# Two half transfers change places, and three weight pieces are loaded as 8 and 120 rows

## The chip, the cores and the metric

The kernel runs on one core of a Trainium2 chip. A core has a matrix engine (TensorE; PE in the profile, with its weight loads as PEld), a vector engine (VectorE, DVE), an activation engine (ScalarE, ACT), a general engine (GpSimd, POOL) and a small engine that mostly issues transfers (SyncE, SP). Transfers are carried by the core's 16 DMA engines. The metric is the device time of one execution in microseconds, the median over the runs; lower is better.

## The reference

Attention with a threshold, and after it a feed-forward block with a SoLU activation. All is in single precision; the two weight matrices come in double precision.

```python
# q, k, v: (8 batches, 8 heads, 576 tokens, 64)
scores = q @ k.T / sqrt(64)
thresh = max(scores, axis=-1) - tau
scores = where(scores >= thresh, scores, -1e9)
attn = exp(scores - max(scores)); attn /= sum(attn) + 1e-9
x = (attn @ v)            # heads side by side: (4608 tokens, 512)
h = x @ w_in              # (4608, 1024)
solu = h * softmax(h)
ln = (solu - mean) / sqrt(var + 1e-6) * g_ln
out = ln @ w_out          # (4608, 512)
```

## The kernel before

**Slots and units.** The attention is cut into slots. A slot is one batch, one kind (0 and 1 are the two large parts of the tokens, 2 the rest), one pair of heads and one of two row blocks r. Two slots, r = 0 and 1, make a unit. A loop runs over rounds; round `rnd` writes down the scores of slot `rnd` and, besides, the later steps of earlier slots. There is no scheduler behind it: each engine gets its instructions in the order in which this loop writes them.

In a slot, TensorE makes the scores (`scores`, L480), VectorE the row minima (`maxes`, L502), ScalarE applies the threshold (`ramp`, L517) and the exponential (`exps`, L526), and GpSimd divides by the sums (`normalise`, L533 to L536). In the next round VectorE transposes the two blocks into a tile `T` (`blocks`, L548).

**The transfers of a unit.** When both slots of a unit are in `T`, three DMAs on SyncE's queue bring it into the tile `wT`, in which the heads are arranged as the next product needs them: L557 takes the 64 middle partitions of `T` into all 128 partitions of `wT` (its second group of columns), and L559, in a loop over `half`, takes partitions 0 to 31 of `T` into rows 0 to 63 of `wT` (half 0) and partitions 96 to 127 into rows 64 to 127 (half 1). L564 is the form of kind 2, with four transfers. There are two buffers of `wT`.

**The product behind them.** Three or four rounds later (`LAG_PV`) `attend_steps` writes the matmuls of `pv`, L590: for each of nine blocks m first those that read rows 0 to 63 of `wT` (u = 0), then those of rows 64 to 127 (u = 1). `attended` copies the result on ScalarE (L622) into `xh`, from which the feed-forward steps go on: `ff_h` (L645, L655), `ff_max` and `ff_exp`, `ff_stats`, `ff_swap` (four DMAs, L737), `ff_turn` and `ff_o` (L760). In the steady part the rounds interleave this work with the scores on TensorE.

**The weights.** The double-precision weights are loaded in 16 pieces of 128 rows of 512 numbers (4096 bytes a row) by `weight_load(x)`, L275: pieces 0 to 2 on ScalarE's queue, the others on SyncE's. `weight_a`, `weight_b` and `weight_c` turn a piece into single precision on VectorE, ScalarE and GpSimd, one piece a round in rounds 0 to 15; `weight_d` (L332) brings the output weights with their row halves changed round into a second place. In round r, behind the unit's transfers, piece r + 4 is loaded (in round 0 pieces 3 and 4, in round 11 none, in round 12 piece 15). So pieces 5, 8 and 11 are issued in rounds 1, 4 and 7, and between them stand loads of the values `v` (L177, L182).

**SyncE's queue.** SyncE issues its DMAs one after the other, each when what it needs is there. The completion of DMAs is told by eight semaphores in turn, and a DMA waits until the one eight before it, which used the same semaphore, has landed.

Of the kernel before, what the change touches and what calls it, by code (L numbers as in the profile page):

```python
# [16 lines left out]
P = 128  # L17
# [3 lines left out]
def kernel(  # L21
# [236 lines left out]
    def piece(x):  # L258
        if x < 2 * NP:
            c, hf = divmod(x, 2)  # L260
            cols = slice(512 * hf, 512 * hf + 512)
            return w_in[P * c : P * c + P, cols], w1[:, c, cols], W_UNIT
        c = x - 2 * NP
        return w_out[P * c : P * c + P], w2[:, 2 * c], gs[:, c : c + 1]
# [4 lines left out]
    def weight_load(x):  # L269
        raw = work.tile(  # L270
            [P, 512], I64 if wide else F32, tag=("xh2", "xh3", "uT", "xh1")[x % 4 if x < 15 else 0],
            bufs=1, name="raw"
        )
        queue = nc.scalar if x < 3 else nc.sync
        queue.dma_start(out=raw, in_=piece(x)[0])  # L275
        raws[x] = dict(raw=raw)

    def weight_a(x):
# [261 lines left out]
    def blocks(s):  # L540
        b, kind, hp, r = slots[s]
        key = (b, kind, hp)
        if r == 0:
            units[key] = dict(T=work.tile([P, NB, 2, 2, 32], F32, tag="T", name="T"))
        u = units[key]
        T = u["T"]
        for h, w in enumerate(live.pop(s)["w"]):
            nc.vector.transpose(out=T[:, :, r, h, :], in_=w)  # L548
        if r == 0:
            return  # L550


        T = T.rearrange("p (c m) r h x -> p c (m r h x)", c=2)
        u["wT"] = wT = work.tile([P, 2, NK, 2, 2, 32], F32, tag="wT", bufs=2, name="wT")
        to = wT.rearrange("p g m r h x -> p g (m r h x)")
        if kind < 2:
            nc.sync.dma_start(out=to[:, 1], in_=T[32:96])  # L557
            for half in range(2):
                nc.sync.dma_start(out=to[ROWS[half], 0], in_=T[96 * half : 96 * half + 32])  # L559
            return  # L560
        for g in range(2):
            for half in range(2):
                of = 64 * half + 32 * g
                nc.sync.dma_start(out=to[ROWS[half], g], in_=T[of : of + 32])  # L564
# [303 lines left out]
    with tc.manual_schedule():  # L868
        nc.scalar.dma_start(out=tau_t, in_=tau.partition_broadcast(P))
        load_qk(0, 0)  # L870
        weight_load(0)
        constants()
        for x in range(1, 3):
            weight_load(x)
# [23 lines left out]
        while True:  # L898
# [135 lines left out]
            if rnd - 1 in live:  # L1034
                blocks(rnd - 1)
# [10 lines left out]
            if rnd in pieces:  # L1046
                x = pieces[rnd]
                weight_b(x)
                for y in {0: (3, 4), 11: (), 12: (15,)}.get(x, (x + 4,)):
                    if y < len(pieces):  # L1050
                        weight_load(y)
                if x + 1 < len(pieces):
                    weight_a(x + 1)
# [39 lines left out]
```

## Time and profile before

| what | value |
|---|---|
| median of 3 runs | 868.01 us (865.58 to 868.37) |
| profiled execution | 869.02 us, its span 867.2 us |
| mean granted TensorE clock | 0.976 |
| instructions | 36122 |
| TensorE busy | 822.9 us, 95% of the span |
| SyncE's DMA queue (q1) | 82416 packets, 164.25 MB |
| `wT<-T` issues of L557 and L559, and of L564 | 64 of 576 KB; 160 of 288 KB |
| loads of weight pieces (`raw`) on SyncE | 5 and 8 of 512 KB |

Times in the views are in microseconds from the start of the span. A line of the view in order of time gives the start, the length, the engine, the line of the kernel, what is done, how often, and in brackets how long the engine stood idle before and what ended that. "SPq" is an issue on SyncE. The granted clock is the share of full speed that TensorE was allowed. A pass is one matmul instruction as the profile counts it.

### The profile page before, as it was taken

What the parts mean: (1) busy time and instruction counts of PE and PEld (TensorE: products, weight loads), DVE (VectorE), ACT (ScalarE), POOL (GpSimd) and SP (SyncE); (2) the same over time, 40 slices, a digit from 0 to 9 for tenths busy, and PEclk for the clock granted to TensorE, in tenths of its full rate; (3) what the DMA queues carried; (4) which work ended last, traced back from release to release, by engine and by line L of the source; (5) the groups of instructions that cost most, each with busy time, mean ns of one, the idle gap of its engine ahead of it and who ended that gap; (6) DMA issues with size and microseconds to landing.
All of it is one profiled execution on the core that took longest, in us unless ns stands there. A gap on an engine that the chain in (4) does not pass through costs nothing.

```text
span 867.2 us, 36122 instructions
## 1 busy us (share of the span) xinstructions
PE 822.9 (95%) x15361; PEld 605.8 (70%) x15361; DVE 681.7 (79%) x1248; ACT 573.6 (66%) x1153; POOL 500.2 (58%) x938
## 2 busy tenths in 40 slices
PE   5668799989999999999999999999999999999997
PEld 3446466667677776899777766777777777777655
DVE  4988878878788888888888887888788887787361
ACT  5877876667677767777666766777677776776121
POOL 2886656556756666565656665565666655555120
PEclk9769999999999999999999999999999999999999
DMA  8999887998888878898888787888788787655312
GB/s 256 252 251 227 191 210 181 210 236 210 215 206 226 208 183 214 208 221 203 196 207 225 207 187 185 217 220 207 183 230 229 197 192 180 163 136 139 69 38 62
DMA packets 83712, 168.54 MB, mean 194 GB/s; under 512 B 15448, under 2 KB 45152, under 8 KB 83552
## 3 DMA queue, kind: packets, MB, share of 16 engines
q1 hardware_dynamic: 82416, 164.25, 76.3%
q8 instruction: 120, 1.97, 1.0%
q10 hardware_dynamic: 1136, 2.00, 0.7%
q14 instruction: 40, 0.33, 0.1%
HBM read 46.14 MB, written 9.44 MB: 64 GB/s over the span
## 4 chain that ended last, share of the span: by engine, by line
PE 79%; DMA 8%; DVE 4%; ACT 4%; SPq 2%; issue 2%; POOL 1%; ACTq 0%; DVEq 0%
PE o_ps L760 26%; PE h_ps L655 20%; PE pv L590 14%; PE s_ps L480 14%; DMA wT<-T 6%; PE h_ps L645 3%; ACT w L517 1%; DVE w L502 1%; ACT w L526 1%; DVE T L548 1%; DMA q<-in_q_dram 1%; DMA qT<-flip 1%; SPq L564 1%; DMA k<-in_k_dram 1%; SPq L559 0%
## 5 line engine op out<-in xcount | busy, mean ns | idle before, releaser
L760 PE MATMUL o_ps<-w,uT 64*64 64x256 f32 x4608 | 271.6, 378 | 1.2 <-ACT xe L622 0.6
L502 DVE CUSTOM_DVE_ANT_0 w<-s_ps,tau_t 128x576 f32<-128x576 f32 x280 | 200.0, 751 | 90.0 <-PE s_ps L480 61.6
L517 ACT ACTIVATE w<-s_ps,nth 128x576 f32<-128x576 f32 x280 | 196.9, 739 | 107.0 <-DVE nth L502 89.6
L760 PEld LDWEIGHTS o_ps<-w,uT 64*64 64x64 f32 x4608 | 212.7, 134 | 66.1 <-ACT xh L622 12.1
L536 POOL TENSOR_SCALAR w<-w,sm 128x576 f32<-128x576 f32 x288 | 222.1, 783 | 14.3
L548 DVE STREAM_TRANSPOSE T<-w 128x576 f32<-128x576 f32 x288 | 207.6, 755 | 20.6 <-POOL w L536 19.1
L655 PE MATMUL h_ps<-w,xh 64*64 64x512 f32 x1856 | 221.0, 589 | 0.1
L526 ACT ACTIVATE w<-w,ntau 128x576 f32<-128x576 f32 x288 | 219.7, 767 | 0.0
L590 PEld LDWEIGHTS pv<-wT,v 64*64 64x64 f32 x5760 | 175.2, 138 | 45.4 <-issue 24.5
L480 PE MATMUL s_ps<-kT,qT 64*64 64x64 f32 (+1 forms) x2048 | 177.1, 422 | 13.3 <-ACT w L517 10.9
L590 PE MATMUL pv<-wT,v 64*64 64x128 f32 (+1 forms) x5760 | 178.0, 266 | 10.9 <-DMA wT<-T 7.8
L655 PEld LDWEIGHTS h_ps<-w,xh 64*64 64x64 f32 x1856 | 118.0, 133 | 78.8 <-issue 45.7
L533 POOL TENSOR_SCALAR sm<-sm 128x2 f32<-128x2 f32 x144 | 37.0, 257 | 201.8 <-ACT w L526 198.5
L534 POOL TENSOR_TENSOR sm<-sm,mone 128x2 f32<-128x2 f32 x144 | 108.7, 755 | 12.0
L480 PEld LDWEIGHTS s_ps<-kT,qT 64*64 64x64 f32 x2048 | 73.0, 139 | 21.7 <-ACT w L517 15.7
L622 ACT COPY xh<-pv 128x256 f32<-128x256 f32 x64 | 25.1, 393 | 82.4 <-PE pv L590 82.4
L721 ACT ACTIVATE V<-u,nb,rs 128x1024 f32<-128x1024 f32 x36 | 44.7, 1241 | 39.3 <-POOL nb L711 32.4
L747 DVE STREAM_TRANSPOSE uT<-V 128x1024 f32<-128x1024 f32 x36 | 44.2, 1227 | 18.1 <-DMA V<-u 17.7
L526 ACT ACTIVATION_READ_ACCUMULATOR w<-w,ntau 128x1 f32 x288 | 55.6, 193 | 0.0
L685 DVE TENSOR_TENSOR u<-h_ps,u 128x1024 f32<-128x1024 f32 x36 | 42.8, 1190 | 9.8 <-ACT u L679 9.8
L726 DVE TENSOR_SCALAR u<-u,rs,nb 128x1024 f32<-128x1024 f32 x36 | 35.3, 982 | 17.6 <-ACT V L721 17.6
L670 DVE TENSOR_REDUCE hm<-h_ps 128x1 f32<-128x1024 f32 x36 | 42.9, 1192 | 4.8 <-PE h_ps L645 2.7
(90 smaller groups left out, 568.1 us busy)
## 6 DMA issues: line engine op xcount, KB each, us to landing
wT<-T SPq DMA_DIRECT2D x160, 288.0 KB, 6.7
wT<-T SPq DMA_DIRECT2D x64, 576.0 KB, 5.4
V<-u SPq DMA_DIRECT2D x144, 64.0 KB, 3.3
out_dram<-ob SPq DMA_DIRECT2D x71, 128.0 KB, 2.5
q<-in_q_dram SPq DMA_DIRECT2D x24, 288.0 KB, 5.7
qT<-flip SPq DMA_DIRECT2D x48, 144.0 KB, 4.2
k<-in_k_dram SPq DMA_DIRECT2D x24, 288.0 KB, 6.1
kT<-flip SPq DMA_DIRECT2D x48, 144.0 KB, 3.9
```

Source lines behind the costliest of these rows:

```text
L480: nc.tensor.matmul(out=ps[h][ROWS[y], ks], lhsT=lhsT, rhs=d["kT"][ROWS[h], ks], start=True, stop=True,)
L502: nc.vector.tensor_tensor_reduce(out=w, in0=ps[:, 0:S], in1=(zero if loose else tau_t).to_broadcast([P, S]), scale=1.0, scalar=BIG, op0=AL ...
L517: nc.scalar.activation(out=d["w"][x], in_=d["w"][x] if d["loose"] else d["ps"][x][:, 0:S], func=AF.Prelu, bias=d["nth"][x], scale=-1.0, al ...
L526: nc.scalar.activation(out=w, in_=w, func=AF.Exp, bias=ntau, scale=1.0, accum_out=sm[:, x : x + 1])
L534: nc.gpsimd.tensor_tensor(out=sm, in0=sm, in1=mone, op=ALU.pow)
L536: nc.gpsimd.tensor_scalar(out=w, in0=w, scalar1=sm[:, x : x + 1], scalar2=1.0, op0=ALU.mult, op1=ALU.mult)
L548: nc.vector.transpose(out=T[:, :, r, h, :], in_=w)
L590: nc.tensor.matmul(out=to, lhsT=d["v"][ROWS[u], (h0 + h - u) % 4 if b > 1 else h0 + h, m ^ 4 * u if m < 8 and b < 2 else m,], rhs=rhs, sta ...
L655: mm = nc.tensor.matmul(out=h[ROWS[y], f], lhsT=x[ROWS[r], c, ROWS[y]], rhs=w1_parts[ROWS[r], c, part ^ r], start=part == 0 and c == 0, st ...
L721: nc.scalar.activation(out=V, in_=u, func=AF.Identity, bias=nb, scale=rs)
L747: nc.vector.transpose(out=uT, in_=d["V"].rearrange("p y (m x) -> p m y x", x=32))
L760: nc.tensor.matmul(out=d["o"][ROWS[z], 512 * (r ^ other) : 512 * (r ^ other) + 256], lhsT=d["uT"][ROWS[r], m].rearrange("p y x -> p (y x)" ...
```

## The change

In `weight_load`, pieces 5, 8 and 11 are loaded by two DMAs, one of rows 0 to 7 and one of rows 8 to 127, instead of one DMA of 128 rows. In `blocks`, the loop over the two half transfers of a unit runs over (1, 0) instead of (0, 1). Both stay on SyncE's queue. No other instruction changes its place on its engine.

```diff
@@ weight_load
         queue = nc.scalar if x < 3 else nc.sync
-        queue.dma_start(out=raw, in_=piece(x)[0])
+        for rows in (slice(0, 8), slice(8, P)) if x in (5, 8, 11) else (slice(0, P),):
+            queue.dma_start(out=raw[rows], in_=piece(x)[0][rows])
         raws[x] = dict(raw=raw)
@@ blocks
         if kind < 2:
             nc.sync.dma_start(out=to[:, 1], in_=T[32:96])
-            for half in range(2):
+            for half in (1, 0):
                 nc.sync.dma_start(out=to[ROWS[half], 0], in_=T[96 * half : 96 * half + 32])
             return
```

## The prediction

> **What bounds the kernel now.** I read four views, in this order: the page's parts 1 and 2, the busy time by stretches, the instructions of TensorE in order of time, and the issues of SyncE in order of time.
>
> ```profile
> PE 822.9 (95%) x15361; PEld 605.8 (70%) x15361; DVE 681.7 (79%) x1248; ACT 573.6 (66%) x1153; POOL 500.2 (58%) x938
> PEclk9769999999999999999999999999999999999999
> DMA  8999887998888878898888787888788787655312
> ```
>
> TensorE is busy for 822.9 of 867.2 us, so 44.3 us of it stand still. The DMA engines are busy nearly throughout, and the granted clock is low early on.
>
> ```profile
> 43.00:65.00 22.00, 15.26 (x208) 9.15 (x208) 18.49 (x39) 15.62 (x32) 18.04 (x22) 0.69 1.05 250
> 65.00:87.00 22.00, 19.44 (x314) 14.47 (x316) 18.21 (x38) 16.02 (x31) 14.09 (x18) 0.92 0.99 226
> ...
> 300.00:400.00 100.00, 100.00 (x1937) 81.55 (x1933) 84.11 (x152) 69.58 (x140) 60.70 (x119) 1.00 0.84 208
> ```
>
> The columns are the stretch, its length, the busy time of PE, PEld, DVE, ACT and POOL, the granted clock, the DMA share and GB/s. By the whole table of these stretches 37.1 us of TensorE's idle time lie before 200 us, 2.4 us between 200 and 820, and 4.9 behind. From 200 us on a transfer that lands a little sooner or later finds TensorE occupied, and nothing is to be won or lost there. The change is decided before 200 us, where the DMA share is about 1.0 from 43 to 87 us.
>
> ```profile
> 58.04 0.69 PE L590 MATMUL pv<-wT,v 64*64 64x128 f32 x4 [1.80 <-DMA wT<-T]
> 59.08 3.89 PE L590 MATMUL pv<-wT,v 64*64 64x128 f32 x66 [0.35 <-DMA wT<-T]
> 66.93 0.44 PE L590 MATMUL pv<-wT,v 64*64 64x128 f32 x4 [2.16 <-DMA wT<-T]
> 68.00 3.58 PE L590 MATMUL pv<-wT,v 64*64 64x128 f32 x66 [0.63 <-DMA wT<-T]
> 80.13 2.23 PE L590 MATMUL pv<-wT,v 64*64 64x128 f32 x70
> 174.84 0.54 PE L590 MATMUL pv<-wT,v 64*64 64x128 f32 x4 [1.41 <-DMA wT<-T]
> 176.15 3.18 PE L590 MATMUL pv<-wT,v 64*64 64x128 f32 x66 [0.78 <-DMA wT<-T]
> ```
>
> These are the places that the change touches. A unit's attention product starts when its first half transfer has landed, does 4 passes, and waits again for the second half. The waits are 2.15 us at 58, 2.79 at 67 and 2.19 at 175. The same product takes 59 ns a pass at 59 us (3.89 / 66) and 32 ns at 80 us (2.23 / 70): the granted clock is 0.50 in the first place and 1.00 in the second. The trace's clock records stand in steps of about 3.4 us, and half-speed steps lie at 54.1 to 64.3, 67.7 to 71.1 and 176.9 to 180.3 us, the last two at the end of such a wait. One step costs 1.7 us of work (half of 3.4).
>
> ```profile
> 45.27 0.59 SPq L557 DMA_DIRECT2D wT<-T  x1
> 46.38 3.00 SPq L559 DMA_DIRECT2D wT<-T  x2
> 50.66 1.84 SPq L275 DMA_DIRECT2D raw<-in_moe_w_out_dram  x2
> 54.63 0.58 SPq L557 DMA_DIRECT2D wT<-T  x1
> ```
>
> SyncE's DMAs carry eight completion semaphores in turn, so at most eight are under way, and here that binds. The second L559 of this pair starts at 48.84 us; the transfer eight before it (raw piece 8) landed at 48.83, by the trace's semaphore records, from which the other landings below are too.
>
> **The profiled execution** took 869.02 us: a span of 867.2 and 1.8 around it, 1.0 above the median of 868.01. I work out differences and put them on the median.
>
> **The swap.** Nothing is added or removed; 64 units issue the half with rows 64 to 127 first and rows 0 to 63 second. The matmuls begin with rows 0 to 63, so the 4 passes that now fill the gap between the two landings come after it. Where TensorE waits for landings, that is 4 x 59 ns = 0.24 us at half clock, 4 x 32 = 0.13 at full. It counts at 58 and 67 (there only the last remains, since each start is a landing) and at 175: 0.24 + 0.24 = +0.48 us. In the other units both halves land before TensorE reaches them (2.4 us of idle from 200 to 820 us cover them): nothing, and up to 0.13 for each of the four later waits (2.8 us in all), +0.5, if that cover is gone.
>
> **The split.** Pieces 5, 8 and 11 each become two issues on SyncE: three DMAs more. An issue took 0.33 us at the shortest (L275), so 1.0 us of SyncE's time. Queued behind them are value loads and, in rounds 4 and 7, the next unit's L557. That L557 starts at 45.27 and 54.63 after waiting for VectorE's transposes (the wait at 53.5 lasts 1.1 us), which covers 0.33. In DMA bytes nothing changes.
>
> What changes is who carries them. The one 8-row transfer of before, the gain rows, left exactly eight packets of 512 B in the trace; 64- and 128-row ones report from sixteen engines. So 8 rows land on eight engines, one each, and these do one row more than the rest. A row is a 4096 B packet: mean 233 ns in 22 to 43 us, 242 in 43 to 65. The queue does not run empty from 21 to 97 us, so three rows accumulate: a lag of about 3 x 0.24 = 0.7 us. No row of before shows how 120 rows are spread. Between bounds of one engine spared 8 rows (-1.9 us on it) and the rows falling on eight engines as 15 each (+7 x 0.24 = 1.7 us on them), I take about 8 rows each, the row nearest to it being 128 over sixteen.
>
> The Trainium skill ("DMA: Bandwidth & Descriptors", section on why a DMA increments its semaphore by 16) gives as the engine count the largest number up to 16 that divides the rows, taken from the lowest engine: 8, and 15 for 120 rows, so the last engine gets none. By that, engines 0 to 7 do 9 rows, 8 to 14 do 8; no transfer of 120 rows is in this trace to agree or not.
>
> **What the lag is worth.** The packets of a unit, 4608 B, take 178 ns at the tenth percentile and 310 ns on average from 43 to 87 us: they disturb each other, by 132 ns each. An engine moves 8 in L557 and 4 in each half. When all engines are in the same half, they crowd on the same 32 source and 64 destination rows; when half of them are a half transfer behind, they are on different rows. The order (1, 0) suits this if the lagging engines are those that work on rows 0 to 63 in L557: the others are by then on the upper rows. The trace does not name engines; that the eight are these is assumed. The full excess of the halves is 8 x 132 = 1.06 us a unit; a lag of three rows is 3 x 4096 / 4608 = 2.7 of the 4 packets of a half, so up to two thirds is saved, 0.7 us a unit. Four units are issued between 24 and 55 us with lags of 1, 1, 2 and 3 rows, which save 0.25, 0.25, 0.5 and 0.67 of 1.06: together 1.8 us at the landing at 68. Against it stand the lagging engines' own extra rows. What lands last is one engine: at the unit of 45.27 fourteen engines report by 54.8 us for the first half and two at 56.8 and 57.9, after single 16 KB instruction packets at 36.67 and 44.08 had held them up. If that engine is not a lagging one, 1.8 us stay; that is what I take, as these packets fall on single engines whichever they are. The bounds are 0 (the spread of 2.4 us among the other engines already mixes the halves) and 4.9 (both waits gone).
>
> **The clock.** A wait of 2.79 - 1.8 leaves about 1 us at 67 instead of 2.8. The half-speed step at 67.7 follows the longest wait, and full speed holds from 71.1 to 95 us, where TensorE's waits stay under 1 us until 93. I take this step as gone: -1.7. Bounds: -3.4 (the one at 176.9 too) and +3.4 (two more).
>
> The page's rule for authors speaks against the change: two transfers to disjoint partition halves serialize, so one should be used ("DMA: Bandwidth & Descriptors", rules for kernel authors). By it the lag brings nothing, and the sum would be only the swap, +0.5.
>
> **Sum:** +0.5 (swap) + 0 (issues, covered) - 1.8 (landings) - 1.7 (clock step) = -3.0 us: 865.0.
>
> **Rivals.**
> - *Faster, as above* (0.45). From -2.6 to all that the waits hold: 4.9 at 58 and 67, a clock step of 1.7, and half of 2.2 at 175, so -7.7.
> - *The lag is lost* (0.25). For it: the spread of 2.4 us among engines is over three times the lag. Against: the queue never empties until 97 us. Swap alone, +0.5, and a clock step either way of part size: 866 to 870.
> - *The eight slots bind* (0.17), slower. Each split takes one slot of eight. In the unit at 45 us its last half then waits for the next landing, 50.59 instead of 48.83: 1.8 us later. It decides once the slowest engine has less than 1.8 us of work queued then; it had 57.9 - 50.6 = 7.3 us by its landings, which speaks against it, but the later, less burdened units have not. Price 1.8 at 59 plus a clock step 1.7 plus the swap 0.5: +4.0, 872.0.
> - *The last engine is one of the laggards* (0.13), slower. Its three rows add 0.7, no contention is saved on it, one more clock step 1.7, swap 0.5: +2.9, 870.9.
> - *The split does something else*, within these: 120 rows on eight engines would add 1.7 us a piece, and belongs to the last.
>
> **Numbers.** 0.3% is 2.6 us, about what a measurement of this kernel tells from no change (its three runs span 2.8). Faster 0.45, same 0.25, slower 0.17 + 0.13 = 0.30. The likeliest case gives 865.0, its own range 860.3 to 865.4. For 8 in 10 the range reaches from 860.5 to 872.5: one in ten of the gains is larger, and past +4.5 lie two more clock steps with the slots.
>
> **What would show it.** Right: the rows at 58 and 67 show one start of 70 passes with a wait under 2 us, mean 4608 B packet below 300 ns from 43 to 87 us, and no half-speed step at 67 to 71. The swap is wrong if the 4 passes still start apart. The slots: L559's second issue later than 50 us. It would be wrong if the idle time before 200 us grows over 37.1 us, or if the span changes while the stretch from 200 to 820 us does.

## The result, and the profile after

| | before | changed |
|---|---|---|
| median | 865.13 us (861.11 to 868.37, 20 runs) | 871.58 us (864.50 to 875.78, 20 runs) |
| ratio changed to before | | 1.0067 [1.0048, 1.0086] |
| profiled execution, its span | 869.02, 867.2 us | 872.06, 870.3 us |

The change makes the kernel slower by 0.67%, about 5.8 us. (The ratios here and below are those of all runs of a comparison, with 95% intervals; they are not quotients of two medians.) The forecast was 865.0 us against 868.01; it had the wrong sign. The result lies in the range given and near the two slower rivals (872.0 and 870.9), but what those rivals were to show is not what happened, as told below; that it falls inside is luck. Two things in the first column matter below. One kernel scatters by about 10 us from one execution to the next. And the execution of before that the prediction was read from, 869.02 us, lies above all 20 of these runs.

The page of the changed kernel, parts 1 and 2:

```profile
PE 822.8 (95%) x15361; PEld 618.2 (71%) x15361; DVE 681.8 (78%) x1248; ACT 574.2 (66%) x1153; POOL 500.0 (57%) x938
PEclk9868999999999999999999999999999999999999
DMA  8999786897888878878888887888788887655312
```

TensorE is busy as long as before (822.8 for 822.9 us), so all of the difference is idle time. Busy time by stretches of the changed kernel, with the columns of the prediction's table (stretch, length, then PE, PEld, DVE, ACT, POOL, the granted clock, DMA share, GB/s):

```profile
45.00:110.00 65.00, 50.92 (x884) 31.54 (x888) 55.03 (x110) 48.39 (x107) 45.88 (x62) 0.82 0.95 222
110.00:200.00 90.00, 81.94 (x1636) 56.53 (x1632) 68.41 (x135) 59.86 (x125) 51.17 (x97) 0.96 0.84 205
250.00:820.00 570.00, 568.16 (x10761) 451.36 (x10757) 464.96 (x833) 388.17 (x766) 339.37 (x659) 1.00 0.80 196
```

From 250 to 820 us TensorE stands still for 1.8 us, as good as never. What was lost was lost before. The instructions of TensorE in order of time, changed kernel, at the places that the prediction spoke of:

```profile
57.37 4.23 PE L591 MATMUL pv<-wT,v 64*64 64x128 f32 x72 [1.55 <-issue]
66.63 4.12 PE L591 MATMUL pv<-wT,v 64*64 64x128 f32 x72 [3.64 <-DMA wT<-T]
178.65 3.71 PE L591 MATMUL pv<-wT,v 64*64 64x128 f32 x72 [3.40 <-DMA wT<-T]
```

The attention product has one start now in place of two, as the change of order says, but the wait in front of it is 3.64 us at 67 us and 3.40 at 178, where before had 2.79 and 2.19 with four passes in between. (The wait at 57 us is named "issue"; by the semaphore records the last half transfer landed at 57.28, 0.09 us before the start, so it is a wait for `wT` too.) One wait is new, in the feed-forward block's second product:

```profile
120.19 1.42 PE L761 MATMUL o_ps<-w,uT 64*64 64x256 f32 x10 [3.57 <-DMA w<-w]
```

Against the profile of before, the starts of the exponentials slot by slot are level (within 0.4 us) or up to 1.6 us earlier until 118 us, then 3.3 us later at this wait. My first theory was therefore: the later half transfers make the last weight copy (`w<-w`, L332 of before) late. It was one execution against one execution, and it fell.

### The profile page after: what moved, and what is told of

The parts are those of the page before. It is cut to its first block, busy times and chain, and to the rows that moved or that the text cites. A ratio compares the mean times of both kernels' runs of the same rounds, so it can differ in the third digit from the quotient of the medians.

```text
span 870.3 us, 36122 instructions
## 1 busy us (share of the span) xinstructions
PE 822.8 (95%) x15361; PEld 618.2 (71%) x15361; DVE 681.8 (78%) x1248; ACT 574.2 (66%) x1153; POOL 500.0 (57%) x938
## 4 chain that ended last, share of the span: by engine, by line
PE 83%; DMA 5%; DVE 4%; ACT 3%; issue 2%; SPq 1%; POOL 1%; ACTq 0%; DVEq 0%
PE o_ps L761 26%; PE h_ps L656 23%; PE pv L591 15%; PE s_ps L481 15%; PE h_ps L646 3%; DMA wT<-T 1%; ACT w L518 1%; DVE w L503 1%; DVE T L549 1%; ACT w L527 1%; DMA w<-w 1%; DMA raw<-in_moe_w_out_dram 1%; DMA ends<-in_q_dram 1%; DVE w L307 1%; DMA k<-in_k_dram 1%
## 5 line engine op out<-in xcount | busy, mean ns | idle before, releaser
L761 PE MATMUL o_ps<-w,uT 64*64 64x256 f32 x4608 | 273.5, 377 | 5.0 <-DMA w<-w 3.6
L761 PEld LDWEIGHTS o_ps<-w,uT 64*64 64x64 f32 x4608 | 214.1, 133 | 67.2 <-ACT xh L623 12.0
L591 PEld LDWEIGHTS pv<-wT,v 64*64 64x64 f32 x5760 | 178.2, 138 | 40.4 <-issue 13.0
L481 PE MATMUL s_ps<-kT,qT 64*64 64x64 f32 (+1 forms) x2048 | 181.2, 424 | 13.0 <-ACT w L518 10.7
L591 PE MATMUL pv<-wT,v 64*64 64x128 f32 (+1 forms) x5760 | 178.2, 266 | 11.2 <-DMA wT<-T 7.3
L656 PEld LDWEIGHTS h_ps<-w,xh 64*64 64x64 f32 x1856 | 121.9, 133 | 75.4 <-issue 27.9
L481 PEld LDWEIGHTS s_ps<-kT,qT 64*64 64x64 f32 x2048 | 75.5, 140 | 22.6 <-ACT w L518 15.3
```

Source lines behind the costliest of these rows:

```text
L481: nc.tensor.matmul(out=ps[h][ROWS[y], ks], lhsT=lhsT, rhs=d["kT"][ROWS[h], ks], start=True, stop=True,)
L591: nc.tensor.matmul(out=to, lhsT=d["v"][ROWS[u], (h0 + h - u) % 4 if b > 1 else h0 + h, m ^ 4 * u if m < 8 and b < 2 else m,], rhs=rhs, sta ...
L656: mm = nc.tensor.matmul(out=h[ROWS[y], f], lhsT=x[ROWS[r], c, ROWS[y]], rhs=w1_parts[ROWS[r], c, part ^ r], start=part == 0 and c == 0, st ...
L761: nc.tensor.matmul(out=d["o"][ROWS[z], 512 * (r ^ other) : 512 * (r ^ other) + 256], lhsT=d["uT"][ROWS[r], m].rearrange("p y x -> p (y x)" ...
```

## The experiments

Each kernel was run beside before on the same chip, the groups of kernels on different chips; so each has its own median of before. An interval of 0.002 to 0.004 to each side is what this kernel's scatter leaves.

### One half of the change at a time

Only the order of the half transfers:

```diff
-            for half in range(2):
+            for half in (1, 0):
```

> Only the two half transfers change places; the weight pieces are loaded whole. Theory A (the loss arises at one place, about 120 us, where the output product waits 3.57 us for the last copy of the output weights, and it is the order of the halves that makes that copy late, since by 103 us all sixteen engines of the split kernel report within 0.4 us of each other): +4 to +6 us, with a wait of the output product on the weight copy of 2 us or more near 120 us. Theory B (the split is the cause, by its lag, its slots or the moved timing): -1 to +1 us and no such wait. Theory C (the two only do harm together): -1 to +1 us here and with the split alone. Theory D (the order of the halves slows the steady part): +4 to +6 us, with the difference to the kernel before growing after 200 us.

Measured: 867.65 against 863.62 us, ratio 1.0058 [1.0035, 1.0082]. Only the split of pieces 5, 8 and 11:

```diff
-        queue.dma_start(out=raw, in_=piece(x)[0])
+        for rows in (slice(0, 8), slice(8, P)) if x in (5, 8, 11) else (slice(0, P),):
+            queue.dma_start(out=raw[rows], in_=piece(x)[0][rows])
```

> Only the three pieces are loaded as 8 and 120 rows; the halves stay in the order 0, 1. Theory A (the order of the halves makes the last weight copy late at 120 us): -1 to +1 us. Theory B (the split is the cause): +4 to +6 us. Theory C (only both together): -1 to +1 us. Theory D (steady part): -1 to +1 us.

Measured: 867.77, ratio 1.0038 [1.0013, 1.0063]. Each half costs something by itself; neither needs the other. The two together (1.0067) stand below their sum (1.0096), but the difference is within the intervals.

### The late weight copy

The last weight copy, `weight_d(15)`, is issued ahead of the unit's transfers of its round, in the changed kernel and in before:

```diff
+            if rnd == 16:
+                weight_d(pieces[15])
             if rnd - 1 in live:
                 blocks(rnd - 1)
...
-                weight_d(pieces[rnd - 1])
+                if rnd < 16:
+                    weight_d(pieces[rnd - 1])
```

> The changed kernel, with the two copies of the last output weight piece issued ahead of the transfers of the unit in round 16 instead of behind them. If the late copy at 120 us is the loss (theories A, B and C differ only in what makes it late), the wait of the output product on it goes and the time is that of the kernel before, -2 to +1 us; the same unit's transfers start up to 1 us later and are not waited for. If the loss is spread over the steady part (theory D), +4 to +6 us stay.

> The kernel before, with the two copies of the last output weight piece issued ahead of the transfers of the unit in round 16. In its profile the last copy landed at 116.8 us, just ahead of its use near 117.7, so the profiled execution has nothing to gain: -1 to +1 us if that is typical, -1 to -3 us if other executions of the kernel before do wait there.

Measured: changed kernel with the copy first 870.41, ratio 1.0076 [1.0035, 1.0118]; before with the copy first 864.60, 0.9996 [0.9974, 1.0018]. The wait at 120 us is gone and nothing is seen to be won back. So that wait of 3.57 us was not what the change costs. What surprised was the profile of the second: its span is 860.5 us, and it is before in all but that copy. By about 115 us it runs 6.4 us ahead of the profile of before. The profile I had predicted from was a late one.

### How much a single profile says

The kernel before and the changed kernel once more, unchanged.

> The kernel before, unchanged, beside itself: what a comparison of this kind gives for no change (ratio 1.000, interval about 0.002 to 0.003 to each side), and a second profiled execution. If the execution that the prediction was read from (869.0 us) was a late one, this one shows a shorter span than 867.2 us, and the awaited transfers at 58 and 67 us end less than 4 us behind the median engine.

> The changed kernel, unchanged: ratio 1.005 to 1.009 as before, and a second profiled execution. If the wait of 3.57 us for the last weight copy at 120 us belongs to the change, it is here again; if it was one late engine of one execution, TensorE waits under 1 us there.

Measured: before against itself 1.0004 [0.9980, 1.0029]; changed 869.89, 1.0074 [1.0045, 1.0102]. Stretches of before, second profile (span 864.6 us), columns as above:

```profile
45.00:110.00 65.00, 53.59 (x932) 37.51 (x936) 58.22 (x114) 51.67 (x114) 48.94 (x65) 0.84 0.96 228
110.00:200.00 90.00, 85.31 (x1678) 57.40 (x1672) 72.78 (x143) 62.65 (x130) 53.52 (x103) 0.98 0.86 212
250.00:820.00 570.00, 568.55 (x10778) 437.09 (x10771) 461.74 (x827) 384.43 (x762) 333.93 (x652) 1.00 0.78 194
```

and of the changed kernel, second profile (span 868.1 us):

```profile
45.00:110.00 65.00, 48.36 (x884) 28.92 (x888) 54.72 (x109) 48.13 (x104) 45.98 (x62) 0.87 0.99 221
110.00:200.00 90.00, 82.87 (x1676) 56.64 (x1672) 71.12 (x140) 62.19 (x132) 52.24 (x100) 0.98 0.87 211
250.00:820.00 570.00, 568.98 (x10786) 462.89 (x10782) 464.04 (x832) 386.71 (x764) 337.80 (x657) 1.00 0.79 195
```

With the profiles of the two copy-first kernels there are three profiles of each kind. TensorE's idle time, length of the stretch less its busy time:

| us idle in | 45 to 110 | 110 to 200 | 200 to 250 | 250 to 820 |
|---|---|---|---|---|
| before; again; copy first | 13.9; 11.4; 11.1 | 5.2; 4.7; 6.4 | 0.2; 1.6; 0.5 | 2.1; 1.5; 1.2 |
| changed; again; copy first | 14.1; 16.6; 15.8 | 8.1; 7.1; 8.4 | 1.1; 2.2; 0.6 | 1.8; 1.0; 0.5 |
| difference of the means | +3.4 | +2.4 | +0.5 | -0.5 |

The means differ by 6.3 us from 45 to 250 us, which is the size of the timed loss, and by -0.5 behind. This is where the time went, as far as three profiles of each tell (within each three, 45 to 250 us differs by 1.6 and 2.8 us). Added up over all stops of more than 0.15 us from 45 us on, and averaged over each three, the idle time in front of the attention product (L590 of before, L591 of changed) grows from 7.7 to 10.9 us, that in front of the feed-forward block's second product (L760, L761) from 1.5 to 3.8, that in front of the scores hardly (10.3, 10.6). The new wait at 120 us was 1.17 us in the second profile of the changed kernel, and there is none in its copy-first form. The second profile of the changed kernel:

```profile
58.37 4.23 PE L591 MATMUL pv<-wT,v 64*64 64x128 f32 x72 [2.76 <-issue]
68.22 4.12 PE L591 MATMUL pv<-wT,v 64*64 64x128 f32 x72 [4.24 <-DMA wT<-T]
117.74 0.86 PE L761 MATMUL o_ps<-w,uT 64*64 64x256 f32 x10 [1.17 <-DMA w<-w]
```

In the second profile of before (below) the product at 57 us does not wait at all and the one at 64.5 us waits 2.66 + 0.68 us. In the first it had waited 2.15 and 2.79.

```profile
56.79 3.97 PE L590 MATMUL pv<-wT,v 64*64 64x128 f32 x70
64.51 0.44 PE L590 MATMUL pv<-wT,v 64*64 64x128 f32 x4 [2.66 <-DMA wT<-T]
65.63 2.73 PE L590 MATMUL pv<-wT,v 64*64 64x128 f32 x66 [0.68 <-DMA wT<-T]
```

### Where the order of the halves costs

The order (1, 0) in the two units waited for at 58 and 67 us alone, and its complement (the first expectation says 34 other units; there are 62). Each line of the cuts in this part stands for `for half in range(2):`.

```diff
+            for half in (1, 0) if key in ((0, 0, 2), (0, 0, 3)) else (0, 1):
```

> Before with the order (1, 0) of the half transfers in two units alone: the two of the first batch whose attention product waits for wT at about 58 and 67 us; all 34 other units keep (0, 1). With every unit changed the time rose by 4.0 to 4.8 us and the mean granted clock fell from 0.983 to 0.979, which is 3.8 us of the span. Theory R (the loss arises in the ramp: without the four passes that the first half allows, TensorE stands idle in one piece and more half-speed steps of the clock follow, 1.7 us each): the whole loss is here, 3 to 5 us over before (ratio 1.0035 to 1.006), clock 0.979. Theory S (the order of the halves slows the steady part, where nothing waits visibly): under 1 us (ratio below 1.0015), clock 0.983.

> The complement: the order (1, 0) in every unit but those two. Theory R: within 1 us of before, clock 0.983. Theory S: 3 to 5 us over before, clock 0.979. A share in each would say that the first two units, or the unit waited for at 175 us, carry a part.

Measured: the two units 1.0017 [0.9985, 1.0049], all others 1.0055 [1.0030, 1.0081]. Theory R, that the whole loss sits at the two visible waits, falls: 0.30% or more is there without them (the lower end of the second interval), by the point value nearly all of it. A share of the two units is not ruled out (up to 0.49%). The others were divided further, in this order: the rest of the first batch; all later batches; of these the two units that TensorE is seen waiting for at 175 and, in some profiles, 233 us; the other units of later batches.

```diff
+            for half in (1, 0) if b == 0 and key not in ((0, 0, 2), (0, 0, 3)) else (0, 1):
+            for half in (1, 0) if b > 0 else (0, 1):
+            for half in (1, 0) if key in ((1, 0, 3), (2, 0, 0)) else (0, 1):
+            for half in (1, 0) if b > 0 and key not in ((1, 0, 3), (2, 0, 0)) else (0, 1):
```

> Order (1, 0) in the first batch's other units alone: the first two and the four of kind 1, not the two waited for at 58 and 67 us, and no unit of a later batch. The order in all units but those two cost 4.8 us. Theory F (the loss arises in the first 130 us, where the queue is full and transfers of wT, weights and inputs follow each other): 3 to 5 us over before, clock below 0.981. Theory L (it arises in later batches, where profiles show one wait at 175 us and one at 233 us grown by 0.4 to 1 us each): within 1.3 us of before.

> The complement among later batches: order (1, 0) in every unit of kinds 0 and 1 of batches 1 and up, none in the first. Theory F: within 1.3 us of before. Theory L: 3 to 5 us over. What the profiles show for sure is 0.5 us at 175 and 0.5 us at 233 us, with a half-speed step more or less (1.7 us), so 1 to 2.7 us would be the bare sum of passes that no longer fill the gap.

> Order (1, 0) in two units of the later batches alone: those whose transfers TensorE is seen waiting for at 175 and 233 us. All later batches together cost 3.5 us. Theory of the awaited units (order matters only where TensorE waits): 2 to 3.5 us over before here. Theory of the whole stream (each unit's order costs a little through what follows it in the queue): within 1.3 us of before.

> The complement: order (1, 0) in all units of later batches except those two, which TensorE is nowhere seen waiting for. Theory of the awaited units: within 1.3 us of before. Theory of the whole stream: 2 to 3.5 us over before.

Measured: rest of the first batch 1.0021 [0.9993, 1.0049]; all later batches 1.0044 [1.0009, 1.0080]; of these the two units that TensorE is seen waiting for 1.0002 [0.9978, 1.0026], the others 1.0025 [1.0000, 1.0049]. The point values of the three disjoint groups (two units, rest of the first batch, later batches) add up to 0.0082 where the whole order costs 0.0058, within their intervals. What can be held to: most of the order's cost, by the point values, does not come from the units whose waits are visible, and no group stands out as carrying it alone. That it is spread over many units is the likeliest reading, and is not shown; which unit costs how much these runs do not tell.

### The passes, or the transfers?

For TensorE the order of the halves can be copied without touching a transfer: turn its loop over u round (alone: g4), so that its first passes read the half that lands last. Done together with the order (1, 0), the first passes read the first half again (f3).

```diff
             for m in range(NK):
-                for u in range(2):
+                for u in range(2) if kind == 2 else (1, 0):
```

> Order (1, 0) in every unit, and in the attention product of kinds 0 and 1 the loop over u turned round as well, so that the first passes read the half of wT that now lands first. Theory R: the four passes fill the gap between the two landings again, so all of the loss is gone: within 1 us of before, clock 0.983. Rival: the order of the transfers itself (which rows the queue sends first) makes landings later: 3 to 5 us over before whatever TensorE's order, clock 0.979.

> No transfer is changed: the loop over u of the attention product of kinds 0 and 1 is turned round, so that its first passes read the half of wT that lands last. For TensorE that is the same lack of four passes between the two landings as the changed order of transfers gives. Theory of the passes: 4 to 5 us over before, as with the order of transfers. Theory of the transfers (which rows are sent first is what matters): within 1.3 us of before. With both turned round 3.2 us were lost, so a share of each is possible.

Measured: passes turned round alone 1.0008 [0.9977, 1.0039]; together with the transfers 1.0037 [1.0011, 1.0063]; transfers alone, from above, 1.0058. The order alone exceeds the passes alone by 0.0050, give or take 0.0039 (the two half widths in quadrature), and exceeds both together by 0.0021, give or take 0.0035. So the order in which the rows are sent costs by itself: with TensorE's passes fitted to it at least 0.11% stays (the lower end of the interval), by the point value 0.37 of 0.58%. What TensorE does in the gap may have a share; these runs do not tell it from nothing. In the profile with the passes alone the products at 59 and 68 us look just like those of the changed kernel:

```profile
59.28 4.22 PE L590 MATMUL pv<-wT,v 64*64 64x128 f32 x72 [3.11 <-DMA wT<-T]
68.42 3.49 PE L590 MATMUL pv<-wT,v 64*64 64x128 f32 x72 [3.49 <-DMA wT<-T]
```

and its median is close to that of before (863.66 and 863.06 us). Longer waits at these two places are no proof of a longer time.

The order leaves a mark on the transfers of others. By the traces' packet records from 240 to 700 us, packets of 2048 B (the feed-forward block's swap, L737) take 126.5 to 129.7 ns on average in the eight profiles that have the order (1, 0) in later batches, and 120.5 to 125.2 ns in the ten that have not, the passes-only kernel among them; packets of 4608 B take 299.1 and 295.8 ns, with an overlap between the two groups. The last two kernels below fit as well (126.4 with the order, 123.7 without). There this is hidden, as TensorE hardly waits; it shows that the order of the halves changes how long packets of other transfers take. That the same thing makes the loss before 250 us was not shown: from 110 to 240 us the two groups' packets of 2048 B do not differ (130.2 and 129.3 ns).

### What the split does

First the same three pieces as 64 and 64 rows (the same number of DMAs), then the split of 8 and 120 rows on pieces 12, 14 and 15, each by itself:

```diff
+        for rows in (ROWS if x in (5, 8, 11) else (slice(0, P),)):
+        for rows in (slice(0, 8), slice(8, P)) if x in (12, 14, 15) else (slice(0, P),):
```

> Before with pieces 5, 8 and 11 loaded as 64 and 64 rows in place of 8 and 120: the same three more DMAs, issues and completion semaphores, but every engine gets the same number of rows, so that none lags. The split of 8 and 120 rows alone cost 3.2 us of mean time (ratio 1.0038), with the clock at 0.979. Theory of the lag (uneven engines): within 1 us of before, clock 0.983. Theory of the slots (one more of eight semaphores taken per split, later issues): 3 us over before as with 8 and 120, clock 0.979.

> Before with the split of 8 and 120 rows moved to pieces 12, 14 and 15, which are loaded at 59, 71 and 84 us, behind the transfers of wT that TensorE waits for at 58 and 67 us; 5, 8 and 11 are whole again. Theory of the place (the split hurts because it stands ahead of the awaited transfers in the queue): within 1.3 us of before, clock 0.983. Theory of the uneven engines anywhere in the ramp: 3 us over before, as with 5, 8 and 11, clock 0.979.

Measured: 64 and 64 rows 1.0017 [0.9993, 1.0042]; late pieces 1.0017 [0.9992, 1.0041]. Both are smaller than the 1.0038 of the split itself and neither is told from nothing, nor from 1.0038. The traces say more than the times. By the semaphore records, in the last half transfer of the unit waited for at 67 us, issued at 55.2 to 56.9 us in all of these:

| kernels | first engine lands | ninth of sixteen | last |
|---|---|---|---|
| 8 and 120 rows in 5, 8, 11 (changed twice, copy first, split alone) | 61.9 to 62.7 | 65.2 to 66.8 | 66.6 to 68.2 |
| 64 and 64 rows | 61.6 | 62.6 | 65.9 |
| whole pieces there, loaded as in before (13 profiles) | 60.9 to 62.3 | 61.5 to 63.9 | 63.4 to 69.2 |

With the uneven split one engine alone is ahead, by 2.8 to 4.1 us of the ninth (in the changed kernel the reports begin with 61.96, 63.89, 63.94 and 63.98 us), and the middle of the field is 1.3 to 5.3 us later than with whole pieces, with no overlap between the groups. The last landing, which is the one that TensorE waits for, lies within the range of the others. Packets of 4096 B from 43 to 65 us take 275 to 292 ns in these four against 203 to 264 in the thirteen, those of 4608 B 314 to 344 against 299 to 323. So the crowding was not thinned out as forecast; by the packets of 4096 B it grew. A piece in two DMAs of even halves has 271 and 309 ns, so part of the longer 4096 B packets may come with two DMAs; the late middle engine does not. How the late middle engine makes the end later was not shown.

Nor do the three splits add up. In these four profiles the first engine leads the second by under 0.5 us in the value loads behind piece 5. In the last half transfer of the unit issued at 45 us, behind piece 8, the lead is 0.3 to 0.6 us (1.9 in the second profile of the changed kernel). In that of the unit issued at 55 us, behind piece 11, it is 1.8 to 3.0 us: about the 2.2 us that 8 packets of 0.28 us make, not the 6.7 of 24. In the unit issued at 66 us it is 0.0 to 0.4 us, 1.1 with the split alone. Where piece 11 comes only at 59 us, in the last kernel below, the transfer of the table has no such lead: the first, ninth and last report come at 61.2, 62.1 and 63.5 us.

### What stands ahead in the queue

If the backlog sets the waits at 58 and 67 us, loading pieces 8 to 14 one round later should shorten them.

```diff
-                for y in {0: (3, 4), 11: (), 12: (15,)}.get(x, (x + 4,)):
+                for y in {0: (3, 4), 4: ()}.get(x, (x + 4 - (x > 4),)):
```

> Before, with weight pieces 8 to 14 loaded one round later each, so that one piece of 512 KB less (about 2 us of the queue at 250 GB/s) stands ahead of the two transfers of wT that TensorE waits for at 58 and 67 us. The order of halves and the rows are those of before. Theory of the backlog (what stands ahead of the awaited transfers sets the loss in the ramp): those waits shrink by 1 to 2 us each, the time by 1 to 4 us (ratio 0.995 to 0.999). Rival: the waits of the ramp are set by something else, or the pieces now come too late for their own use: no gain, or up to 5 us slower.

> The changed kernel (order (1, 0), pieces 5, 8 and 11 as 8 and 120 rows) with pieces 8 to 14 one round later as well. The changed kernel stood at 1.0067 and 1.0074 of before. Theory of the backlog: the later pieces win back part of it, ratio 1.001 to 1.005. Rival: 1.006 or more.

Measured: before with later pieces 1.0007 [0.9983, 1.0031], changed with later pieces 1.0040 [1.0021, 1.0059]. The profile of the first:

```profile
61.52 0.44 PE L590 MATMUL pv<-wT,v 64*64 64x128 f32 x4 [0.77 <-DMA wT<-T]
62.75 2.07 PE L590 MATMUL pv<-wT,v 64*64 64x128 f32 x66 [0.80 <-DMA wT<-T]
...
86.58 0.49 PE L345 MATMUL s_ps<-ident,ends 64*64 64x64 f32 x8 [5.28 <-DMA ends<-in_q_dram]
```

In this profile the wait at 62 us is 1.57 us in place of 3.34 in the second profile of before, and the unit's product ends about 3.5 us earlier, as the theory has it; but before with the copy first, with no piece moved, has 1.88 us there, so one profile does not show that the moved pieces did it. And it brings nothing: at 86.6 us TensorE waits 5.28 us for the rows `ends` of the next batch's inputs. They were issued on the same queue at 76.55 us, behind a weight piece at 73.61 among others, and landed at 86.53. The lead is given back there. In the three profiles of before the same rows landed at 86.99, 85.15 and 83.00 us, and TensorE waited for them 0.05 us at most; whether the moved pieces made them late this one profile does not tell. Without moved pieces much the same shows in the profile with the order changed in all units but two, which was 2.4 us ahead of before with the copy first at 72 us and 3.0 behind it by 105, after these stops (rows of TensorE, VectorE and ScalarE):

```profile
83.39 0.34 PE L345 MATMUL s_ps<-ident,ends 64*64 64x64 f32 x8 [2.13 <-DMA ends<-in_q_dram]
...
92.32 0.87 DVE L286 TENSOR_SCALAR em<-raw 128x512 int32<-128x512 int32 x1 [2.22 <-DMA raw<-in_moe_w_out_dram]
93.23 0.72 ACT L291 ACTIVATE em<-em,lim 128x512 int32<-128x512 int32 x1 [3.82 <-DVE em L286]
...
96.94 0.48 PE L345 MATMUL s_ps<-ident,k 64*64 64x64 f32 x4 [4.08 <-ACT kT L407]
```

The first stop is the next batch's inputs, the second a weight piece: it was issued at 79.58 us behind a unit whose halves stand in the order (1, 0), landed at 92.23, and held up VectorE, through it ScalarE, and through ScalarE's copy into `kT` TensorE. In before with the copy first the unit's last half landed at 87.98 us (here 90.03) and the piece at 90.33. This is one way in which a later transfer reaches TensorE where it waits for no `wT`; that it is the order's doing one profile of each does not show.

For the changed kernel the later pieces may win back 0.3%, at the edge of what the intervals tell. None of the kernels run is faster than before.

## Why the prediction was wrong, point by point

- **What bounds the kernel: right in the main.** It said that nothing is won or lost from 200 us on, and that idle time before 200 us above 37.1 us would prove it wrong. The two profiles of the changed kernel have 40.0 and 44.0 us there, and from 250 to 820 us nothing was lost.
- **The waits it was read from: not typical.** The profiled execution was taken as 1.0 us above the median of three runs. Against 20 to 35 runs per comparison, with medians from 862.9 to 865.1 us, it is some 4 to 6 us late, and the two waits of 2.15 and 2.79 us at 58 and 67 us, on which the gains rested, were partly this execution's own. The second profile of before has 0 and 3.34 us, that with the copy first 0.64 and 1.88. Beside that first profile the changed one does land its transfers earlier (57.28 for 59.04 us, 66.59 for 67.95), which looks like the forecast come true; beside the second, 57.38 and 65.58, it does not.
- **The swap, +0.5: a failed step, by what it put at nothing.** The passes alone cost 0.8 us of the mean (863.68 to 864.48), not told from nothing and in line with +0.48. But the order of the halves costs 0.58%, 5.0 us, by the point values mostly through the transfers themselves, which the step had put at nothing ("in the other units ... nothing"). Its upper bound of +0.5 for the hidden units was far too small, because it priced passes and not the order on the queue.
- **The split's issues, 0: open.** 64 and 64 rows, the same number of issues and semaphores, cost 0.17% with an interval that reaches from -0.07 to +0.42.
- **The lag, -1.8: a failed step, in sign.** The split by itself costs 0.38%, 3.3 us, and no gain is seen. How the rows are shared out was right in its first half: the 8-row piece reports from eight engines, the 120-row piece from fifteen. But that relieves one engine of 8 rows a piece, the bound that had been set aside, and what that engine gains does not build up over three pieces. Behind piece 11 it runs 2.8 to 4.1 us ahead of the middle engine, and the middle engine comes later. The mark named for the gain, mean 4608 B packets below 300 ns from 43 to 87 us, is missing: 309 and 335 ns in the two profiles, 311 and 309 in those of before. Whether the uneven shares or the three further DMAs carry the cost is open, since 64 and 64 rows are not told from 8 and 120. The Trainium skill ("DMA: Bandwidth & Descriptors", section on why a DMA increments its semaphore by 16) gives 8 and 15 engines for 8 and 120 rows; the traces agree with both counts, and which engines these are they do not name.
- **The clock step, -1.7: wrong.** It did not go. The changed kernel has two half-speed steps from 65.8 to 72.6 us, two and one in its further profiles (from 66.7 and 67.1 us), where the three profiles of before have one each. Over the timed executions the mean granted clock is 0.983 in before (30), 0.978 in the changed kernel (20), 0.979 with either half alone (12 each). Of spans of 862 and 869 us that is 14.7 and 18.9 us not granted; as idle time counts in it too, the 4.2 us are an upper bound for what the clock took.
- **The rivals.** The slots: named to show as a second L559 later than 50 us. It was issued at 47.18, earlier than before, so this is not what happened; the result's nearness to 872.0 is no support. A laggard as last engine: the last is only 1.4 us behind the ninth there, where before had 4.05, and it is the middle that is late; as the traces do not name engines, whether the last one is a laggard they do not tell. The page's rule that two transfers to disjoint partition halves serialize was set against the gain, and the gain did not come; no run here tests that rule.
- **What no step had:** a transfer that lands earlier in this stretch need not bring the end nearer. The next batch's inputs and the next weight piece are on the same full queue, and where TensorE came early they stopped it at 83 to 97 us.

What stays open: through which wait the order of the halves reaches the end, unit by unit, and whether a late single engine is more frequent with it or only later.

## What to carry to other kernels

Where executions of one kernel scatter by 10 us, the waits of one profile are a draw: read the same waits in a second profile before pricing their removal, and set the profiled time against many runs, not three. On a queue that does not run empty for 60 us, an earlier landing may only move the stop to the next thing on that queue; look for that one before counting the gain. Here a split that left one engine without rows put that engine ahead for a while and helped nobody, for the last to land is what counts.

## What the runs showed of the hardware

- **TensorE can stand still in the middle of a product, it seems for its instructions.** In the feed-forward block's second product a stop falls after pass 15, at the same instruction in several kernels, with nothing shown that it waits for. In order of time, in the order-only kernel:

```profile
136.47 1.09 PE L760 MATMUL o_ps<-w,uT 64*64 64x256 f32 x15
139.25 3.02 PE L760 MATMUL o_ps<-w,uT 64*64 64x256 f32 x49 [1.69 <-issue]
```

By the packet records a single 16 KB packet of the instruction queue (q8) landed at 137.72 us, 1.53 before the restart. In all twelve profiles with this stop (0.21 to 1.99 us long) the distance is 1.26 to 1.60 us. In the first two profiles of before there is no stop at this place, in that with the copy first it is 0.42 us, in the three of the changed kernel 0.84 to 1.41 us. The queue carries 120 such packets in an execution. The Trainium skill ("Runtime: NRT & Kernel Launch", section on instruction fetch mechanics) says that an engine's sequencer fetches its instructions by DMA in blocks of 16 KiB and that the cost of crossing a block is mostly hidden; the size agrees with these records, and if the reading is right the stops are what was not hidden. That the wait is for the packet is inferred from the nearly constant distance.
- **A single engine can be late by 4 us for a long time.** In the profile of before the last of sixteen reports of a transfer is 1.5 us behind the ninth at 25 us, 3.4 at 35 us and 4.05 at 56 us, in before with the copy first 0.4, 1.6 and 2.1. How late the last engine was at 56 us goes only in part with the span: among kernels not told from before, the two shortest spans (860.4 and 860.5 us) have this landing at 63.4 and 64.1 us and the three longest (866.7 to 867.4 us) at 68.0 to 68.3, but two of 863.4 and 864.5 us have it at 68.7 and 69.1. That the late engine makes the scatter was not tested.
